# Four interleaved layers (sliding attention, Fourier mixing) on one core: the tables that order both attention layers' half-steps and tails are set anew

## The chip, the core and the metric

The kernel runs on one core of one Trainium2 chip. The core has a matrix engine (PE, with its own queue of weight loads, PEld), a vector engine (DVE), a scalar engine (ACT), GpSimd (POOL), and SP, which only issues transfers. Each engine executes its own instructions in their order in the program and waits at an instruction until what it needs is there. The metric is the time of one execution of the whole program on the device, in microseconds (us); lower is better. Comparisons use the median of several executions.

## What is computed

x has 2048 rows (S) of 640 values (D), in fp32. Four layers are added one after the other: attention A, Fourier mixing B, A, B.

```python
def _A_ref(x, wqkv, wo):
    H = 32; Dh = D // H
    W, dil = 8, 2
    q, k, v = ...                      # from x @ wqkv, 32 heads of 20 values
    idx = pos[:, None] - off[None, :]  # off = 0, 2, .. 14: eight earlier rows
    logits = jnp.einsum("bhsd,bhswd->bhsw", q, kg) * scale
    logits = jnp.where(mask[None, None, :, :], logits, -1e9)
    attn = _softmax(logits, axis=-1)
    o = jnp.einsum("bhsw,bhswd->bhsd", attn, vg)
    return o.transpose(0, 2, 1, 3).reshape(B, S, D) @ wo

def _B_ref(x, ...):
    a = jnp.einsum("bsd,ed->bse", x, dft_hid_re)
    b = jnp.einsum("bsd,ed->bse", x, dft_hid_im)
    return jnp.einsum("ts,bse->bte", dft_seq_re, a) - jnp.einsum("ts,bse->bte", dft_seq_im, b)

x = x + _A_ref(_layernorm(x), A_wqkv, A_wo)
x = x + _B_ref(_layernorm(x), ...)
x = x + _A_ref(_layernorm(x), A_wqkv, A_wo)
x = x + _B_ref(_layernorm(x), ...)
```

## The kernel before

**Products.** A matrix product of fp32 data is done as three products of rounded parts: each operand is kept as a high part (fp32r) and a residue, and high x high, high x residue and residue x high are summed. That is why a projection of a 128-row tile takes 15 matmuls (3 passes of 5 slices of D). To get a tile with D on the partitions, PE transposes it into PSUM (`pc_pe`, L442; `ident` is the identity), ACT casts the result to the high part (`pc_hi`, L446), PE subtracts that high part from what stands in PSUM with a negated identity (`pc_sub`, L450), and ACT or DVE takes the residue out (`pc_lo`, L463 and L465). Between a transpose and its subtraction PE must have other work, or it waits for the cast.

**An attention layer.** The rows are cut into 4 chunks of 4 tiles. `qkv_mm` (L477) projects one tile, for one of four groups of heads, into one of two PSUM banks m0 and m1. ACT evacuates it (`qkv_evac`, L487, L491, L492), and `qkv_store` (L504, L505) writes the keys and values (`kvb`) and the queries (`qb`) of two tiles to DRAM, from the queue of ACT or of SP (`kvq`). For each of 32 units u (a chunk and an eighth of the heads), `q_load` and `w_load` (from SP) bring the queries and the windows of keys and values back; ACT copies the queries (`q_copy`, L530) into a PSUM tile `pq`; DVE multiplies (`qk_mul`, L557) and POOL adds halves (L560); DVE reduces (`qk_red`, L570) and does the softmax (L585 to L595) around ACT's exp (L578); DVE multiplies with the values (`av_mul`, L600) and POOL adds up (`av_tree`, L615 to L617; at the very end DVE shares this). The outputs are transposed as above and multiplied with wo (`wo_mm`, L640); DVE adds the result to x and sums the rows (`wo_add`, L258); ACT takes the variance (L263, L265). The inverse root of the variance comes either from POOL's power (`finish`, L280 and L282, four tiles at once) or from ACT's Ln and Exp (L271, L272), by the table `lno`. Normalisation is on ACT (L297); the cast of the normalised tile to its high part is `ln_hi` (L1044, ACT), its residue `ln_lo` (L1048, on DVE or POOL by the table `lnv`).

**A Fourier layer** starts inside the attention layer before it: `z_mm` (L1123) multiplies normalised tiles with the DFT matrix over the sequence, in thirds of five matmuls, each third a row of the table `z`. The matrix tiles are loaded (`stg<-cst_in`), and their parts made by `c_hi` (L1074) and `c_lo` (L1106), or read back from DRAM (`c_get`). The rest of the layer is eight steps of `pair` with products L1291 and L1190, whose operands DVE and ACT make ready (L1284, L1285), and outputs through `yout` and L331, L342.

**What sets the order.** `layer_a` does not write instructions down directly. It calls `at(step, phase, function, ...)`, which puts the call into a plan. There are about 66 half-steps, two to each unit. The loop that emits them goes through the half-steps, and in each through the phases in the order of one of two strings of `C['ph']` (one up to half-step 47, one from 48 on):

```python
with tc.manual_schedule(engines=ENGINES):
    for s in range(gs[0], last + 1):
        for ph in C["ph"][s >= 48].split():
            for fn, args in plan.pop((s, ph), ()):
                fn(*args)
```

What it emits is the order of all five engines, word for word. `gs` gives the half-step of each `qkv_mm`; `out`, `t2`, `t3` those of the outputs' transposes; `wo`, `w2`, `w3` those of `wo_mm`; `z` those of the thirds (three values to a half-step: phases z0, z1, pe3); `ln` those of the normalisation for the layer after. After the last half-step a string `tail` of letters orders what is left. Entry 0 of `ly` is for the first attention layer (0 to about 400 us), entry 1 for the second (about 865 to 1260 us). At the seam, the first inputs of the second attention layer are made within the last pair of the Fourier layer, at places given by `early`. In the Fourier layers only PE's order is written out (`run`), and the other engines follow a scheduler.

Of the kernel before, what the change touches and what calls it, by code (L numbers as in the profile page):

```python
# [21 lines left out]
H = 32  # L22
# [4 lines left out]
P = 128  # L27
# [25 lines left out]
 'bufs': {'xa': 2, 'qs': 2, 'stg': 2, 'xr': 1},  # L53
 'pad2': 16,
 'ot': ['ot'],
 'wqg': [0, 0, 0, 0, 0, 0, 0, 1, 1, 1, 0, 1, 0, 1, 1, 0, 1, 0, 1, 0],
 'run': [{'pre': [0, 1, 2, 0, 1, 0, 2, 0, 0, 0, 0, 2, 0, 1, 0, 0],
          'post': [5, 1, 1, 2, 1, 4, 0, 5, 0, 7, 0, 3, 0, 4, 1, 5],
          'y': [[3, 4, 5, 6, 8], [9, 13, 14, 14, 15]]},
         {'pre': [6, 0, 1, 2, 4, 3, 0, 4, 0, 6, 0, 0, 2, 0, 0, 0],  # L60
          'post': [0, 0, 2, 2, 0, 4, 0, 0, 0, 0, 1, 0, 4, 0, 4, 3],
# [5 lines left out]
         'ord': [[2, 0, 1, 3, 4, 6, 5, 7], [2, 0, 1, 4, 6, 5, 3, 7], [0, 2, 1, 4, 3, 6, 5, 7]],  # L67
         'out': [20, 23, 27, 32, 36, 40, 44, 47],
         'wo': [21, 22, 26, 26, 29, 30, 33, 34, 38, 39, 42, 42, 45, 47, 49, 49],
         'woph': 'z1',  # L70
         'ln': [40, 43, 44, 47, 53, 53, 55, 55],
         'w2': [52, 53, 54, 55],
         'w3': [60, 61],
         'lnown': [4, 3],
         'z': [148, 149, 149, 151, 151, 156, 156, 157, 157, 159, 161, 162, 167, 168, 170, 171, 171, 173, 174, 174,
               175, 175, 175, 176, 178, 179, 180, 180, 181, 184, 186, 186, 187, 187, 188, 188, 191, 193, 194, 198,
               198, 199],
         'early': [3, 3, 6.5, 8.7, 5, 6, 7, 8.5, 10, 11, 14, 14.1, 8],
# [11 lines left out]
         'ph': ['evac dma peT0 pe hi z0 fin peL z1 red0 pe2 qk dma2 sA sB red1 sC av0 loE sD sE exp actl evacA sF '  # L90
                'evacO av1 qc dmaw dmac actL lnl pe3w dmar misc clo dmas pe3',
                'peT0 evac dma pe hi z0 peL red0 pe2 z1 fin qk dma2 sA av0 sD sE sB red1 evacA sC loE actL sF evacO '
                'exp dmac av1 actl qc dmas misc clo lnl dmar dmaw pe3 pe3w'],
         'xst': 3,
         'xld': 4,
         'lnx': False,
         'lno': [True, False, False, False],
         'whole': [7, 57, 61],
         'lnv': [1, 1, 1, 0, 0, 1, 0, 0, 0, 1, 0, 0, 1, 1, 0, 1],
# [7 lines left out]
         'ord': [[0, 4, 2, 1, 3, 6, 5, 7], [2, 0, 3, 1, 4, 6, 7, 5], [0, 2, 1, 3, 4, 6, 5, 7]],  # L107
         'out': [20, 24, 29, 32, 36, 40, 44, 46],
         'wo': [23, 23, 26, 28, 30, 31, 34, 35, 38, 38, 42, 42, 46, 47, 48, 49],
         'woph': 'z1',  # L110
         'ln': [40, 42, 42, 46, 52, 54, 55, 55],
         'w2': [52, 53, 54, 55],
         'w3': [60, 61],
         'lnown': [4, 2],
         'z': [148, 148, 150, 151, 151, 152, 155, 160, 161, 162, 164, 168, 168, 169, 169, 170, 171, 171, 173, 174,
               175, 175, 177, 178, 178, 179, 179, 180, 181, 183, 185, 185, 186, 186, 187, 188, 188, 188, 191, 192,
               199, 205],
         'early': [5.3, 2.4, 6.1, 8.4, 5.6, 6, 7.3, 8.8, 7.4, 9.0, 13.0, 13.9, 9.3],
         'ym': [-7, 0],
         'ymph': 'pe2',  # L120
         't2': [49, 49, 48, 48, 50, 50, 52, 52],
         't3': [59, 58, 60, 60],
         'wst': [-1, 0, 0, 1, 0, 1, 0, 0, 0, 0, 0, 0, 1, 0, 0, 0],
         'kvq': [1, 1, 1, 0, 0, 0, 0, 0, 1, 0, 0, 0, 0, 1, 0, 0, 1, 0, 0, 0, 0, 0, 1, 0, 0, 0, 0, 0, 0, 0, 1, 0],
         'yd': [1, 1],
         'ymst': [1, 0],
         'cring': ['s3', 's0', 'wa', 's2'],
         'cpe': [0, 0, 0, 0, 0, 0, 0, 0, 0, 0, 0, 0, 0, 0],
         'zla': [0, 0, 2, 0, 1, 0, 1, 1, 1, 1, 0, 1, 0, 2],
         'ph': ['dma peT0 evac hi red0 pe z0 peL qk z1 fin sA pe2 red1 dma2 sB sD sC av0 loE sE clo evacA exp actl '  # L130
                'actL sF evacO av1 qc dmaw dmas misc pe3 lnl dmar dmac pe3w',
                'peT0 red0 evac pe z0 dma hi fin peL sA z1 qk dma2 pe2 sB red1 av0 sD loE evacA sC sE exp actL evacO '
                'sF av1 dmas dmaw qc actl dmar lnl misc pe3w clo dmac pe3'],
         'xst': 3,
         'xld': 4,
         'lnx': True,
         'lno': [False, False, True, True],
         'whole': [32, 61],
         'lnv': [1, 0, 1, 0, 0, 0, 1, 0, 1, 1, 0, 1, 1, 1, 1, 1],
         'kw': {'pc_pe 57': 3, 'pc_pe 54': 1},  # L140
         'tail': 'z68 P H L M2 z67 M3 A2 S2 F2 c14 d14 p14 T2 A3 l2 Z14 z69 S3 F3 c15 d15 p15 T3 l3 G0 G1 G2 Z15 E '
                 'e0 h0 k0 e1 e2 e3 e4 h1 k1'}],
 'xcr': ['stg', 'sg3', 'sg3']}
TA = 65
# [1416 lines left out]
```

## Time and profile before

| what | before |
|---|---|
| median of 3 runs | 1744.4 us (1742.13 to 1746.95) |
| the profiled execution: its time / its span | 1743.01 us / 1741.2 us |
| granted PE clock | 1.0 throughout |
| PE busy | 1717.2 us, 99% |
| DVE, ACT, POOL busy | 78%, 47%, 35% |

The page gives, for each engine, the time in which at least one instruction ran. A row of the timeline has its start, its length, the engine, line, operation, output and inputs, and in brackets how long the engine stood idle before it and what ended this; several like instructions in a row are one row (x4). PE's matmuls overlap, so the distance between starts, not the length, tells what one costs. The table by stretch has for each window the busy time of PE, PEld, DVE, ACT and POOL with the number of instructions, the clock, the share of the DMA engines and GB/s. Whoever wants to know what a change of order is worth looks at two things: where PE is idle and for whom, and how much later than the engine it will meet next it comes there.

### The profile page before, as it was taken

The numbers are of one execution on the slowest core, as the hardware profiler recorded it, in microseconds if no ns is written. First come the engines' busy times: TensorE is split into PE (matmuls) and PEld (weight loads), VectorE is DVE, ScalarE is ACT, GpSimd is POOL, SyncE is SP. The second block draws the span as 40 slices with busy tenths as digits, with TensorE's granted clock in tenths as the row PEclk, the third lists the DMA queues.
The fourth block names the chain that finished last, engine by engine and source line by source line (L and its number), as shares of the span: only waits on it lengthen the run. The fifth ranks groups of instructions, "written<-read, shape, count | busy, mean of one in ns | idle before, by whom it ended". The sixth has DMA issues, their size and how long they took to land. (4 is left out here: it accounts for less than half of the span.)

```text
span 1741.2 us, 26545 instructions
## 1 busy us (share of the span) xinstructions
PE 1717.2 (99%) x8828; PEld 1496.2 (86%) x8828; DVE 1360.1 (78%) x2117; ACT 822.6 (47%) x1810; POOL 616.1 (35%) x574
## 2 busy tenths in 40 slices
PE   9999999999999999999999999999999999999999
PEld 6888888788888888888888889888888888888888
DVE  5999999878767767767639998899787677677673
ACT  5655644654445444445534434445444444443441
POOL 4899999950000000000019997899200000000000
PEclk9999999999999999999999999999999999999999
DMA  6786779969787687687548856698598768867861
GB/s 239 245 291 199 209 231 309 323 222 331 264 262 232 215 275 235 206 279 226 189 156 269 273 163 219 213 312 318 179 349 268 256 205 260 257 208 240 264 203 54
DMA packets 266713, 419.91 MB, mean 241 GB/s; under 512 B 22192, under 2 KB 144560, under 8 KB 266320
## 3 DMA queue, kind: packets, MB, share of 16 engines
q1 hardware_dynamic: 251744, 408.38, 71.1%
q10 hardware_dynamic: 14832, 9.83, 1.8%
q8 instruction: 70, 1.15, 0.3%
q14 instruction: 67, 0.55, 0.1%
HBM read 332.99 MB, written 85.14 MB: 240 GB/s over the span
## 5 line engine op out<-in xcount | busy, mean ns | idle before, releaser
L477 PE MATMUL m<-r,s 128*128 128x512 f32 (+1 forms) x1920 | 429.8, 379 | 1.3 <-DVE r L759 0.8
L477 PEld LDWEIGHTS m<-r,s 128*128 128x128 f32 x1920 | 350.2, 188 | 57.5 <-DVE r L759 1.2
L1284 ACT CAST r<-win 128x512 fp32r<-128x512 f32 x242 | 147.1, 620 | 176.1 <-DVE win L1320 103.2
L1190 PE MATMUL aux<-r2a,zo 128*128 128x320 f32 x768 | 226.0, 309 | 0.0
L557 DVE TENSOR_TENSOR pr<-pq,win 128x1280 f32<-128x1280 f32 x128 | 189.8, 1483 | 37.5 <-PE aux L1190 20.3
L615 POOL TENSOR_TENSOR pr<-pr 128x640 f32<-128x640 f32 x126 | 207.5, 1647 | 30.3 <-DVE pr L600 29.1
L1190 PE MATMUL aux<-pr,zo 128*128 128x320 f32 x704 | 208.0, 309 | 0.0
L560 POOL TENSOR_TENSOR pr<-pr 128x640 f32<-128x640 f32 x123 | 176.3, 1433 | 88.4 <-DVE pr L557 88.4
L1285 DVE TENSOR_TENSOR r<-win,r 128x512 fp32r<-128x512 f32 x242 | 162.8, 688 | 38.5 <-ACT r L1284 37.7
L600 DVE TENSOR_TENSOR pr<-pq,win 128x1280 f32<-128x1280 f32 x128 | 190.3, 1488 | 2.6
L280 POOL TENSOR_TENSOR stats<-stats,mhalf 128x1 f32<-128x1 f32 (+1 forms) x31 | 22.1, 714 | 457.9 <-ACT stats L274 457.8
L1291 PE MATMUL m<-r,r 128*128 128x512 f32 x600 | 152.9, 389 | 0.0
L1190 PEld LDWEIGHTS aux<-r2a,zo 128*128 128x128 f32 x768 | 144.2, 188 | 2.2
L1190 PEld LDWEIGHTS aux<-pr,zo 128*128 128x128 f32 x704 | 132.2, 188 | 2.4
L1291 PEld LDWEIGHTS m<-r,r 128*128 128x128 f32 x600 | 112.2, 188 | 23.5 <-DVE r L1285 0.6
L1291 PE MATMUL t<-r,r 128*128 128x512 f32 x492 | 132.0, 390 | 0.0
L616 POOL TENSOR_TENSOR pr<-pr 128x320 f32<-128x320 f32 x126 | 113.1, 897 | 9.9
L570 DVE TENSOR_REDUCE lg<-pr 128x64 f32<-128x640 f32 (+1 forms) x128 | 107.2, 837 | 10.0 <-POOL pr L560 9.7
L1320 DVE TENSOR_TENSOR win<-win,win 128x512 f32<-128x512 f32 x109 | 74.9, 691 | 48.4 <-DMA win<-cs_in 46.8
L1291 PEld LDWEIGHTS t<-r,r 128*128 128x128 f32 x492 | 92.4, 188 | 19.8
L1123 PE MATMUL m<-s,r 128*128 128x512 f32 x348 | 106.7, 394 | 2.0 <-ACT r L1060 0.9
L1123 PE MATMUL t<-s,r 128*128 128x512 f32 x348 | 105.2, 390 | 0.0
(297 smaller groups left out, 3236.1 us busy)
## 6 DMA issues: line engine op xcount, KB each, us to landing
win<-cs_in SPq DMA_DIRECT2D x346, 256.0 KB, 4.1
r<-xc SPq DMA_DIRECT2D x240, 256.0 KB, 4.2
win<-kvb SPq DMA_DIRECT2D x96, 440.0 KB, 4.7
xa<-cs_in SPq DMA_DIRECT2D x120, 256.0 KB, 4.5
win<-kvb SPq DMA_DIRECT2D x64, 360.0 KB, 6.0
xc<-sg SPq DMA_DIRECT2D x28, 512.0 KB, 4.6
xr<-xs SPq DMA_DIRECT2D x40, 320.0 KB, 3.5
kvb<-stg SPq DMA_DIRECT2D x32, 320.0 KB, 2.7
```

Of the source, the lines that this page charges most:

```text
L477: nc.tensor.matmul(mt[g][:, : GW[q]], st[:, a, k], wq[q][:, b, k], start=n == 0, stop=n == 14)
L557: nc.vector.tensor_tensor(pr, q, wview(u, jp, 0, [[1, FE]]), op=ALU.mult)
L560: nc.gpsimd.tensor_tensor(pv[:, :, 0:10], pv[:, :, 0:10], pv[:, :, 10:20], op=ALU.add)
L570: nc.vector.tensor_reduce(rows(lgs[u], jp), pv.rearrange("p (a h) d -> p a h d", h=HE), axis=AX.X, op=ALU.add,)
L600: nc.vector.tensor_tensor(pr.rearrange("p j w (h d) -> p (j w) h d", d=DH), rows(lgs[u], jp).unsqueeze(3).to_broadcast([P, 2 * W, HE, DH]) ...
L615: g.tensor_tensor(pr[:, :, 0:4], pr[:, :, 0:4], pr[:, :, 4:8], op=ALU.add)
L616: g.tensor_tensor(pr[:, :, 0:2], pr[:, :, 0:2], pr[:, :, 2:4], op=ALU.add)
L1123: self.last = nc.tensor.matmul(self.z[t][k], self.xn[c][:, a, j, k * P : (k + 1) * P], self.ct[s][:, b], start=s == 0 and i == 0, stop=s = ...
L1190: self.last = nc.tensor.matmul(self.ym[e][:, :320], zt[(k, a, ri)][:, j2 * P : (j2 + 1) * P], w[:, e * 320 : (e + 1) * 320], start=(k, a, ...
L1284: nc.scalar.copy(hi, raw)
L1285: nc.vector.tensor_tensor(lo, raw, hi.bitcast(F32), op=ALU.subtract)
L1291: nc.tensor.matmul(bank, w(a, kb), hl[b], start=start and (a, b) == (0, 0), stop=stop and (a, b) == (1, 0),)
```

## The change

Only tables change; no function is touched. In both entries of `ly`, `gs`, `out` or `wo`, `ln`, `z`, `t2`, `early`, `wst` (when a finished x tile is stored), `zla` (how far ahead a DFT tile is loaded), `ph` and `tail` get new values. One swap in `ord` changes the order of two groups of the last chunk's projections in the first layer. `kvq` moves two pairs of stores from ACT's queue to SP's and one the other way. `lnv` moves one residue from POOL to DVE in the first layer and three from DVE to POOL in the second. `lno` makes ACT (Ln, Exp and a small multiplication per tile) instead of POOL finish the statistics of chunk 1 in the second layer. `wqg` sets anew which of DVE and POOL splits some weights (L233: POOL 5 of 25 in place of 6). In `run` some preparations of the Fourier layers' products change their places. The matmuls are the same 8828.

```diff
--- before.py
+++ after.py
@@ -53,92 +53,92 @@
- 'wqg': [0, 0, 0, 0, 0, 0, 0, 1, 1, 1, 0, 1, 0, 1, 1, 0, 1, 0, 1, 0],
...
+ 'wqg': [0, 0, 0, 0, 0, 0, 0, 0, 0, 1, 0, 1, 1, 1, 1, 0, 1, 0, 1, 0],
...
- 'ly': [{'gs': [-7, -6, -5, -4, -3, -2, -1, 0, 1, 2, 3, 3, 4, 5, 5, 6, 6, 7, 8, 8, 9, 11, 11, 12, 13, 13, 14, 15, 16,
...
+ 'ly': [{'gs': [-7, -6, -5, -4, -3, -2, -1, 0, 1, 2, 3, 3, 4, 5, 5, 6, 6, 7, 8, 8, 10, 11, 11, 12, 13, 13, 14, 14, 15,
...
-         'z': [148, 149, 149, 151, 151, 156, 156, 157, 157, 159, 161, 162, 167, 168, 170, 171, 171, 173, 174, 174,
...
+         'z': [149, 149, 150, 151, 151, 155, 156, 156, 156, 157, 161, 162, 165, 168, 170, 171, 172, 172, 173, 173,
...
-         'kvq': [1, 0, 1, 1, 0, 1, 1, 0, 0, 0, 0, 0, 1, 0, 1, 0, 0, 0, 0, 0, 0, 0, 1, 0, 0, 0, 1, 0, 1, 0, 1, 0],
+         'kvq': [1, 0, 1, 1, 0, 0, 1, 0, 0, 0, 0, 1, 1, 0, 1, 0, 0, 0, 0, 0, 0, 0, 0, 0, 0, 0, 1, 0, 1, 0, 1, 0],
...
-                'peT0 evac dma pe hi z0 peL red0 pe2 z1 fin qk dma2 sA av0 sD sE sB red1 evacA sC loE actL sF evacO '
-                'exp dmac av1 actl qc dmas misc clo lnl dmar dmaw pe3 pe3w'],
...
+                'peT0 evac dma pe hi z0 peL red0 pe2 z1 fin qk dma2 sA av0 sD sE sB red1 evacA sC loE actL sF evacO '
+                'exp dmac av1 actl misc qc dmas clo lnl dmar dmaw pe3 pe3w'],
...
-         'lnv': [1, 1, 1, 0, 0, 1, 0, 0, 0, 1, 0, 0, 1, 1, 0, 1],
...
+         'lnv': [1, 1, 1, 0, 0, 1, 0, 0, 1, 1, 0, 0, 1, 1, 0, 1],
...
-                'peT0 red0 evac pe z0 dma hi fin peL sA z1 qk dma2 pe2 sB red1 av0 sD loE evacA sC sE exp actL evacO '
-                'sF av1 dmas dmaw qc actl dmar lnl misc pe3w clo dmac pe3'],
...
+                'peT0 red0 evac pe z0 dma hi fin peL sA z1 qk dma2 pe2 sB evacA red1 sD av0 loE sC exp sE actL evacO '
+                'sF av1 dmas dmaw qc actl dmar dmac lnl misc pe3w clo pe3'],
...
-         'lno': [False, False, True, True],
...
+         'lno': [False, True, True, True],
...
-         'lnv': [1, 0, 1, 0, 0, 0, 1, 0, 1, 1, 0, 1, 1, 1, 1, 1],
...
+         'lnv': [0, 0, 1, 0, 0, 0, 1, 0, 1, 1, 0, 0, 1, 1, 0, 1],
```

Three places in the order. First, PE in the first attention layer at about 84 to 88 us: projections (L477; `s_115`, `s_133` are the transposed tiles 1 and 2), then the transposes of tile 3 (`xa_742`) and their subtraction (L450). Before:

```order
L477 MATMUL m_137_886<-r_0_12_157,s_115_744 128x512 x15
L477 MATMUL m_143_928<-r_0_12_157,s_133_856 128x512 x15
L442 MATMUL xt_975<-ident_69,xa_742 128x128 x4
L442 MATMUL t_153_976<-ident_69,xa_742 128x128
L450 MATMUL xt_975<-s_151_974,nident_74 128x512
L450 MATMUL t_153_976<-s_151_974,nident_74 128x128
L477 MATMUL m_158_1006<-r_0_12_157,s_151_974 128x512 x15
```

Now:

```order
L477 MATMUL m_137_885<-r_0_12_157,s_115_744 128x512 x15
L442 MATMUL xt_955<-ident_69,xa_742 128x128 x4
L442 MATMUL t_150_956<-ident_69,xa_742 128x128
L477 MATMUL m_151_962<-r_0_12_157,s_133_856 128x512 x15
L450 MATMUL xt_955<-s_148_954,nident_74 128x512
L450 MATMUL t_150_956<-s_148_954,nident_74 128x128
L477 MATMUL m_158_1006<-r_0_12_157,s_148_954 128x512 x15
```

The transposes have moved ahead of one burst of 15 projections, and that burst now lies between them and their subtraction. A like move is made at about 108 us.

Second, PE in the same layer at about 324 to 329 us: transposes of an output piece (`zo`) and of a DFT tile just loaded (`stg`), a third of `z_mm` with the DFT tile `wa`, and the subtractions. Before (a second third with `wa` follows, and then the subtractions):

```order
L442 MATMUL aux_585_3695<-ident_69,zo_520_3259 128x128 x3
L442 MATMUL aux_587_3697<-ident_69,stg_3667 128x128 x4
L1123 MATMUL m_496_3155<-wa_3645,r_1_539_3391 128x512
L1123 MATMUL m_497_3156<-wa_3645,r_1_539_3391 128x512
L1123 MATMUL xt_3157<-wa_3645,r_1_539_3391 128x512
L1123 MATMUL t_499_3158<-wa_3645,r_1_539_3391 128x512
L1123 MATMUL t_500_3159<-wa_3645,r_1_539_3391 128x512
```

Now (another third with `wa` stands ahead of these rows):

```order
L1123 MATMUL m_503_3180<-wa_3597,r_1_539_3392 128x512
L1123 MATMUL m_504_3181<-wa_3597,r_1_539_3392 128x512
L1123 MATMUL xt_3182<-wa_3597,r_1_539_3392 128x512
L1123 MATMUL t_506_3183<-wa_3597,r_1_539_3392 128x512
L1123 MATMUL t_507_3184<-wa_3597,r_1_539_3392 128x512
L442 MATMUL aux_585_3706<-ident_69,zo_522_3267 128x128 x3
L442 MATMUL aux_587_3708<-ident_69,stg_3673 128x128 x4
L450 MATMUL aux_585_3706<-s_584_3705,nident_74 128x384
L450 MATMUL aux_587_3708<-s_586_3707,nident_74 128x512
```

Both thirds stand ahead of the transposes, and the subtractions follow right behind them.

Third, ACT in the second attention layer at about 1060 to 1071 us: evacuations of projections (L491, L492), the exp of unit 16 (L578), the normalisation of an input tile (L297) and the copy of the queries (L530). Before:

```order
L491 COPY stg_10690<-m_1515_10650 128x6x80
L492 COPY sg_1457_10255<-m_1515_10650 128x2x16
L491 COPY stg_10740<-m_1524_10696 128x6x80
L492 COPY sg_1528_10739<-m_1524_10696 128x2x16
L578 ACTIVATE lg_10666<-lg_10666 128x128
L297 ACTIVATE xa_10551<-xa_10551,stats_8520 128x640
L530 COPY pq_8726<-qs_10686 128x320
L446 CAST s_1538_10787<-xt_10788 128x512
L446 CAST s_1538_10787<-t_1540_10789 128x128
```

Now:

```order
L491 COPY stg_10672<-m_1513_10631 128x6x80
L492 COPY sg_1453_10212<-m_1513_10631 128x2x16
L491 COPY stg_10672<-m_1522_10676 128x6x80
L492 COPY sg_1453_10212<-m_1522_10676 128x2x16
L578 ACTIVATE lg_10650<-lg_10650 128x128
L297 ACTIVATE xa_10551<-xa_10551,stats_8517 128x640
L491 COPY stg_10774<-m_1524_10696 128x6x80
L492 COPY sg_1533_10773<-m_1524_10696 128x2x16
L530 COPY pq_8726<-qs_10668 128x320
```

The exp and the normalisation have moved ahead of the third evacuation.

More of the change, by code (lines that the diff above doesn't have):

```diff
@@ L55 @@
  'ot': ['ot'],
- 'wqg': [0, 0, 0, 0, 0, 0, 0, 1, 1, 1, 0, 1, 0, 1, 1, 0, 1, 0, 1, 0],
[L57 to L61, printed above, removed]
[4 rows of a table removed]
+ 'wqg': [0, 0, 0, 0, 0, 0, 0, 0, 0, 1, 0, 1, 1, 1, 1, 0, 1, 0, 1, 0],
+ 'run': [{'pre': [3, 1, 2, 0, 1, 0, 2, 0, 0, 0, 0, 2, 0, 1, 0, 0],
+          'post': [3, 2, 1, 0, 1, 4, 0, 5, 0, 9, 0, 1, 0, 4, 3, 3],
+          'y': [[3, 4, 4, 6, 8], [11, 13, 13, 14, 15]]},
+         {'pre': [5, 1, 1, 2, 4, 4, 0, 4, 0, 6, 0, 0, 2, 0, 0, 0],
+          'post': [1, 0, 1, 2, 0, 3, 0, 0, 0, 0, 2, 0, 3, 0, 4, 3],
[4 rows of a table added]
          'tx': [4, 6, 8, 10, 15, 18, 20, 22, 30, 32, 34, 36],
-         'ord': [[2, 0, 1, 3, 4, 6, 5, 7], [2, 0, 1, 4, 6, 5, 3, 7], [0, 2, 1, 4, 3, 6, 5, 7]],
-         'out': [20, 23, 27, 32, 36, 40, 44, 47],
-         'wo': [21, 22, 26, 26, 29, 30, 33, 34, 38, 39, 42, 42, 45, 47, 49, 49],
+         'ord': [[2, 0, 1, 3, 4, 6, 5, 7], [2, 0, 1, 4, 6, 5, 3, 7], [2, 0, 1, 4, 3, 6, 5, 7]],
+         'out': [20, 25, 27, 32, 35, 40, 44, 47],
+         'wo': [21, 22, 26, 26, 29, 30, 33, 34, 38, 39, 42, 42, 45, 46, 49, 49],
          'woph': 'z1',
@@ L89 @@
          'zla': [0, 0, 0, 0, 0, 0, 0, 2, 0, 0, 1, 0, 1, 0],
[L90 to L91 removed]
+         'ph': ['evac dma peT0 pe hi fin z0 peL pe2 red0 z1 qk dma2 sA sB red1 sC av0 loE sD sE exp actl evacA sF '
+                'evacO av1 qc dmaw dmac actL pe3w dmar misc clo lnl dmas pe3',
                 'peT0 evac dma pe hi z0 peL red0 pe2 z1 fin qk dma2 sA av0 sD sE sB red1 evacA sC loE actL sF evacO '
[L93 removed]
+                'exp dmac av1 actl misc qc dmas clo lnl dmar dmaw pe3 pe3w'],
          'xst': 3,
```

34 lines of the change are left out of this document (17 added, 17 removed), and 12 rows, old and new, of the table CFG.

## Prediction

> **What bounds the kernel now.** I read the page's busy times first, then the table by stage, then the waits of the tensor engine, and last the timeline at each of those waits.
>
> ```profile
> span 1741.2 us, 26545 instructions
> PE 1717.2 (99%) x8828; PEld 1496.2 (86%) x8828; DVE 1360.1 (78%) x2117; ACT 822.6 (47%) x1810; POOL 616.1 (35%) x574
> ```
>
> The change leaves all 8828 matmuls in place, so only the 24.0 us in which PE is idle (1741.2 - 1717.2) can go, or grow. The rows by stretch (length, then busy time of PE, PEld, DVE, ACT, POOL, clock) say where they lie:
>
> ```profile
> 325.00:350.00 25.00, 22.72 (x120) 19.25 (x121) 22.30 (x29) 13.60 (x32) 24.06 (x21) 1.00 0.92 323
> 600.00:625.00 25.00, 25.00 (x112) 20.68 (x111) 18.11 (x30) 11.66 (x23) 0.00 (x0) 1.00 0.91 296
> 1150.00:1175.00 25.00, 22.45 (x134) 20.38 (x133) 23.51 (x38) 10.30 (x28) 23.82 (x23) 1.00 0.92 317
> ```
>
> The Fourier layers (600 to 625 stands for them) leave PE no gap. The attention layers do (2.3 of 25 us at 325, 2.6 at 1150), and there DVE and POOL have 22 to 24 of 25 us of work as well. So in these two stages three engines run nearly level, and a matmul moved into a gap pays only as far as the vector work can follow. No PE wait is long; two rows of the list of PE's waits (total, times, longest):
>
> ```profile
> PE aux L450 <- ACT r L446: 1.7, 2, 1.6
> ...
> PE aux L442 <- DMA stg<-cst_in: 1.7, 1, 1.7
> ```
>
> L442 transposes, L446 casts on ACT, L450 subtracts the cast from the transposed piece: a round trip PE to ACT to PE that only other matmuls between the two can cover.
>
> **The first attention layer (0 to 400 us).** The timeline of PE at the waits that the new order touches:
>
> ```profile
> 87.20 0.50 PE L450 MATMUL xt<-s,nident 128*128 128x512 f32 x1 [0.68 <-ACT s L446]
> ...
> 108.39 0.66 PE L442 MATMUL xt<-ident,xa 128*128 128x128 f32 x4 [0.92 <-ACT xa L297]
> ...
> 286.16 0.50 PE L450 MATMUL aux<-wa,nident 128*128 128x512 f32 x1 [0.40 <-ACT wa L446]
> ...
> 287.33 0.66 PE L442 MATMUL aux<-ident,zo 128*128 128x128 f32 x4 [0.46 <-ACT wa L465]
> ...
> 325.94 0.63 PE L442 MATMUL aux<-ident,stg 128*128 128x128 f32 x4 [1.69 <-DMA stg<-cst_in]
> ...
> 332.54 0.62 PE L1123 MATMUL m<-s,r 128*128 128x512 f32 x2
> ...
> 333.68 0.60 PE L442 MATMUL aux<-ident,stg 128*128 128x128 f32 x4
> 334.95 0.50 PE L450 MATMUL aux<-s,nident 128*128 128x512 f32 x1 [0.68 <-ACT s L446]
> ```
>
> At 87.20 the transposes now stand ahead of a burst of 15 matmuls instead of behind it; a 512-wide matmul takes 0.23 us (five of them, one third of a z product, lie between 332.54 and 333.68), so 3.4 us now lie between transpose and subtraction, more than the 0.68 us that were lacking: -0.68. At 108.39 another such burst goes ahead of transposes that wait for the normalised input: -0.92. At 284 to 291 the transposes of two half chunks are merged and a third of a z product is put between: the waits of 0.40 and 0.46 are covered, but the subtraction of the first piece now follows its transposes with only four others between, and a bare round trip costs 0.68 by the 334.95 row, of which the four (0.60 in the 333.68 row, overlapping) cover all but some 0.2: -0.86 + 0.2, about -0.7. At 325.94 two thirds (ten matmuls, 2.3 us) go ahead of the transposes that wait 1.69 us for a constant's load, -1.69; they stood behind these transposes and covered their cast, so that round trip is bare now, +0.68. At 334.95 a third comes between: -0.68. The sum of PE terms is -0.68 - 0.92 - 0.7 - 1.69 + 0.68 - 0.68 = -4.0 us.
>
> They can't all be kept. The stage ends when PE transposes the last attention outputs, and the vector side finishes them only shortly before:
>
> ```profile
> 370.96 0.54 DVE L617 TENSOR_TENSOR zo<-pr 128x160 f32<-128x160 f32 x1
> ...
> 373.26 0.60 PE L442 MATMUL pq<-ident,zo 128*128 128x128 f32 x4
> ```
>
> From 371.50 (370.96 + 0.54) to 373.26 are 1.76 us: PE can come that much earlier and no more, unless DVE ends earlier too. On DVE two things change. The stores of one K/V and Q block (L504, L505) go from ACT's queue to SP's, and behind them ACT copies the q that DVE waits for:
>
> ```profile
> 190.45 0.43 ACTq L504 DMA_DIRECT2D kvb<-stg  x1
> 190.92 0.54 ACTq L505 DMA_DIRECT2D qb<-stg  x1
> ...
> 199.91 1.49 DVE L557 TENSOR_TENSOR pr<-pq,win 128x1280 f32<-128x1280 f32 x1 [1.03 <-ACT pq L530]
> ```
>
> That is at most -0.97 (0.43 + 0.54, within the 1.03). One residue of the next layer's input (L1048, ln_lo) goes from POOL to DVE: +0.82 by the 816 ns row below. DVE's end moves by -0.15, so the cap is about 1.9. I take **-2.0** for this layer; its bounds are 0 (PE's gains are waited off at the next anchor) and -4.0 (every PE term kept). POOL's relief by the same residue is taken as nothing, since the sum at 370.96 is DVE's.
>
> **The second attention layer (865 to 1260 us).** Here the largest edit is on ACT. The exp of unit 16 and a normalisation stood behind an evacuation that waits for PE; they now stand ahead of it:
>
> ```profile
> 1067.04 0.56 ACT L491 COPY stg<-m 128x480 f32<-128x480 f32 x1 [2.75 <-PE m L477]
> ...
> 1067.57 0.32 ACT L578 ACTIVATE lg<-lg 128x128 f32<-128x128 f32 x1
> ...
> 1067.92 0.29 DVE L591 TENSOR_REDUCE pq<-lg 128x16 f32<-128x128 f32 x1 [3.24 <-ACT lg L578]
> ```
>
> So DVE's wait of 3.24 us goes: the evacuation at 1067.04 had kept ACT idle for 2.75 us. Against it, another normalisation of 0.94 us falls out of an idle stretch of ACT into the copy that DVE waits for at 1049.04:
>
> ```profile
> 1045.22 0.94 ACT L297 ACTIVATE xa<-xa,stats 128x640 f32<-128x640 f32 x1
> ...
> 1049.04 1.49 DVE L557 TENSOR_TENSOR pr<-pq,win 128x1280 f32<-128x1280 f32 x1 [2.36 <-ACT pq L530]
> ```
>
> DVE is up by 2.3 us (3.24 - 0.94). Its waits between 1020 and 1120 (total, times, longest) are nearly all for ACT:
>
> ```profile
> DVE pr L557 <- ACT pq L530: 6.1, 5, 2.4
> DVE pq L591 <- ACT lg L578: 4.7, 2, 3.2
> ```
>
> The copies in the first row stand behind evacuations that PE paces, and a DVE that comes earlier waits there longer, so I let most of the 2.3 be waited off. What PE can gain lies at 1148 to 1164:
>
> ```profile
> 1148.37 0.55 PE L442 MATMUL aux<-ident,zo 128*128 128x128 f32 x3 [0.25 <-POOL zo L617]
> ...
> 1156.88 0.50 PE L450 MATMUL aux<-r,nident 128*128 128x256 f32 x2 [1.57 <-ACT r L446]
> ...
> 1163.92 2.32 PE L640 MATMUL aux<-r2a,s 128*128 128x320 f32 x14 [0.98 <-DVE r L258]
> ```
>
> Transposes that waited 0.25 for POOL come later (-0.25). A third of z (five matmuls, 1.1 us) that stood ahead of the 1163.92 row is now ahead of the 1156.88 row: -1.1 there, +1.1 at 1163.92 unless DVE's add (L258) comes earlier. On POOL the two statistics instructions ahead of the half-sums of unit 26, 1.01 and 0.20 us, become small ACT instructions, while three residues go from DVE to POOL. The cap is again the end of the vector side:
>
> ```profile
> 1229.73 0.54 DVE L617 TENSOR_TENSOR zo<-pr 128x160 f32<-128x160 f32 x1
> ...
> 1231.54 0.60 PE L442 MATMUL pq<-ident,zo 128*128 128x128 f32 x4
> ```
>
> It leaves 1.27 us (1231.54 - 1230.27). I take **-1.0**: 0.25 at 1148, and some 0.75 where DVE's lead shortens the 0.98 at 1163.92. Bounds: +1.0 (the third gives 1.1 back and nothing is earlier) and -2.8 (0.25 + 1.57 + 0.98).
>
> The residues have these prices:
>
> ```profile
> L1048 POOL TENSOR_TENSOR r<-r,r x10: 1569/1578/1589, 307.9 to 1201.2; 128x640 fp32r<-128x640 f32 x10
> L1048 DVE TENSOR_TENSOR r<-xa,r x9: 815/816/1273, 237.0 to 1222.4; 128x640 fp32r<-128x640 f32 x9
> L1048 DVE TENSOR_TENSOR r<-r,r x6: 954/1455/2004, 305.0 to 1202.2; 128x640 fp32r<-128x640 f32 x6
> ```
>
> On DVE the same 128x640 takes 0.82 at best and 2.00 at worst, on POOL always near 1.58. I book the three moves in the second layer as -0.82 each for DVE, hidden by the waits above, and as covered on POOL by the 1.21 us of statistics and its slack to 1231.54; without that cover POOL would end 3 x 1.58 - 1.21 = 3.5 us later. The Trainium skill (GPSIMD Engine Reference, Specifications) speaks against such moves: VectorE and GpSimd share the interfaces to SBUF, and DVE instructions with two SBUF inputs contend. The trace bears it out as far as the spread of 0.82 to 2.00 us goes, though no row names the cause.
>
> **Edits taken as nothing.**
>
> ```profile
> L1285 DVE TENSOR_TENSOR r<-win,r 128x512 fp32r<-128x512 f32 x242 | 162.8, 688 | 38.5 <-ACT r L1284 37.7
> ```
>
> The seam (847 to 930) keeps its PE order; the later load and the copy of the first q lie under the Fourier layer's last products. The Fourier layers' own tables move casts and combines of DVE and ACT while PE is busy 25.00 of 25.00; without that cover each late combine would cost its 0.69 us (L1285). The tails move allocations and one load. Their bound is 1 us either way.
>
> **Sum.** -2.0 - 1.0 = -3.0. The profiled execution took 1743.0 us (span 1741.2), so it becomes 1740.0; the median of the runs shown, 1744.4, lies 1.4 above it, which gives **1741.4 us**. About 0.3%, 5.2 us, is what a measurement of this kernel can tell from no change.
>
> **Rivals.**
> First, the caps give way: DVE's lead of 2.3 us survives to 1164 and both sides end earlier, so the PE terms are kept whole: -4.0 - 2.8 = -6.8, 1737.6 us. For it speaks that the 6.1 and 4.7 us of DVE's waits are for ACT, whose order is what changes; against it the 1.76 and 1.27 us.
> Second, slower: in the first layer two pairs of stores go to SP's queue and one leaves it. SP also issues the window loads for DVE's products; a store that waits for its evacuation holds the loads behind it. The loads' landing time, and DVE's wait for them between 50 and 375:
>
> ```profile
> win<-kvb SPq DMA_DIRECT2D x96, 440.0 KB, 4.7
> ...
> DVE pr L557 <- DMA win<-kvb: 0.7, 1, 0.7
> ```
>
> Where a store stands ahead of a load with no lead left, DVE, busy 23 of 25 us, can't catch up: 4.7 for each of two, less the 1.76 of slack, less the 1.0 of the second layer: +6.6, 1751.0. Before, DVE waited for such a load 0.7 us in all, so there was a lead; it decides once the held loads lose more than it.
> Third, contention: each of the three residues moved to POOL stretches a DVE product beside it by 1.18 (2.00 - 0.82), 3.5 together, in place of the -1.0: -2.0 + 3.5 = +1.5, 1745.9. By the skill's rule on the shared interfaces this is what off-loading to POOL would do.
> Fourth, nothing moves, because each PE gain is waited off at the next anchor of DVE (L258) or of a load: 1744.4.
>
> **How the numbers follow.** Forecast 0.36, first rival 0.30, second 0.16, third 0.08, fourth 0.10. The forecast's own range is 1739 to 1744. For the first rival's spread the range goes down to 1735.5 (a further 2.1, DVE's whole lead kept), and up to 1748, which leaves out most of the second. Faster by over 0.3% is under 1739.2: most of the first rival (0.26) and over a quarter of the forecast (0.10), 0.36. Slower by over 0.3% is over 1749.6: the second rival and a little of the third, 0.17. The rest, 0.47, is within.
>
> **What would show it.** In the new trace the waits at 87, 108 and 326 us are gone and new ones of some 0.7 us stand behind the transposes near 285 and 328. DVE's wait of 3.2 us for exp near 1067 is gone, the one near 1049 is longer. PE's total idle is near 21 us. If the gap between the last sums (L617) and PE's transposes at the end of each attention layer has shrunk from 1.8 and 1.3 us to nearly nothing, the cap was real; if it stayed and the end came earlier, the first rival holds. I am wrong on the other side if DVE shows waits of microseconds for `win<-kvb`, or if PE's idle rises over 24 us.

## The result, and the profile after

| | before | changed |
|---|---|---|
| median of 22 runs each | 1742.62 us | 1740.62 us |
| lowest to highest | 1741.09 to 1747.63 | 1739.14 to 1742.87 |
| span of the profiled execution | 1741.2 us | 1739.3 us |

The ratio of changed to before is 0.9984, with a 95% interval of 0.9978 to 0.9991: 2.8 us faster, between 1.6 and 3.8. The two medians are 2.0 us apart. The forecast was 3.0 us. When the changed kernel was timed again (below), the executions with a granted clock of 1.0 alone had medians of 1742.93 before (21 of 33) and 1740.68 changed (8 of 11), so the gain is not one of the clock.

The page of the changed kernel, its first rows:

```profile
span 1739.3 us, 26562 instructions
PE 1718.1 (99%) x8828; PEld 1496.7 (86%) x8828; DVE 1356.2 (78%) x2116; ACT 825.3 (47%) x1818; POOL 616.4 (35%) x573
```

PE is idle for 21.2 us (1739.3 - 1718.1) where it was 24.0. The span fell by less, 1.9 us, since the same 8828 matmuls count as busy for 0.9 us longer (1718.1 - 1717.2). By stretch (length, then busy PE, PEld, DVE, ACT, POOL, clock), two windows of the attention layers:

```profile
325.00:350.00 25.00, 24.09 (x132) 20.43 (x131) 23.61 (x32) 13.02 (x29) 24.05 (x22) 1.00 0.95 348
1150.00:1175.00 25.00, 23.34 (x140) 21.33 (x139) 23.42 (x41) 14.91 (x38) 23.59 (x21) 1.00 1.00 374
```

These windows have gained 1.4 and 0.9 us of PE work (22.72 and 22.45 before). The list of PE's waits (total, times, longest) has another head:

```profile
PE m L477 <- ACT sg L492: 1.5, 1, 1.5
...
PE aux L442 <- DVE r L258: 1.1, 1, 1.1
PE aux L640 <- DVE r L258: 1.1, 1, 1.1
```

None of these three was among the first three of before. The timeline of PE shows where they stand:

```profile
105.68 0.62 PE L477 MATMUL m<-r,s 128*128 128x384 f32 x2 [1.54 <-ACT sg L492]
...
284.18 0.63 PE L442 MATMUL aux<-ident,zo 128*128 128x128 f32 x4 [0.63 <-DVE xa L258]
285.54 0.39 PE L450 MATMUL aux<-ot,nident 128*128 128x256 f32 x1 [0.30 <-ACT s L446]
...
304.43 0.66 PE L442 MATMUL aux<-ident,stg 128*128 128x128 f32 x4 [1.09 <-DVE r L258]
...
326.64 0.60 PE L442 MATMUL aux<-ident,stg 128*128 128x128 f32 x4
327.37 1.05 PE L450 MATMUL aux<-s,nident 128*128 128x384 f32 x2
328.26 0.64 PE L1123 MATMUL m<-wa,r 128*128 128x512 f32 x2
...
333.32 0.39 PE L450 MATMUL aux<-s,nident 128*128 128x512 f32 x1
```

The waits at 87, 108, 326 and 335 us of before are gone. New are the 1.54 at 105.68 and 0.87 more at 304.43. Rows of before to compare:

```profile
304.72 0.66 PE L442 MATMUL aux<-ident,stg 128*128 128x128 f32 x4 [0.22 <-DVE r L258]
...
326.32 0.70 PE L1123 MATMUL m<-wa,r 128*128 128x512 f32 x2
...
328.71 0.56 PE L450 MATMUL aux<-s,nident 128*128 128x384 f32 x2
329.11 0.63 PE L1123 MATMUL m<-wa,r 128*128 128x512 f32 x2
```

The move behind 326 us did bare a round trip, though the row at 327.37 has no bracket. From the four transposes at 326.64 to the next z matmul at 328.26 PE now takes 1.62 us. Before, when other matmuls lay between, the same four transposes took 0.38 (325.94 to 326.32) and the two subtractions 0.40 (328.71 to 329.11). The difference, 0.84 us, is spread over this row and shows only in the distances between starts.

Single profiles differ by some tenths of a microsecond in each layer, so every profile below is read by the same two stretches, between PE instructions that stand at the same place of the program in all of them. Before, the first layer's stretch goes from the subtraction at 58.66 to the z matmul at 384.91, the second layer's from 1138.78 to 1242.89:

```profile
58.66 0.50 PE L450 MATMUL xt<-s,nident 128*128 128x512 f32 x1 [0.68 <-ACT s L446]
...
384.91 1.35 PE L1123 MATMUL m<-s,r 128*128 128x512 f32 x3 [0.59 <-ACT r L1060]
...
1138.78 0.44 PE L450 MATMUL t<-r,nident 128*128 128x384 f32 x1 [0.24 <-ACT r L446]
...
1242.89 0.73 PE L1123 MATMUL m<-s,r 128*128 128x512 f32 x2 [0.29 <-ACT r L1060]
```

In the changed kernel:

```profile
58.64 0.51 PE L450 MATMUL xt<-s,nident 128*128 128x512 f32 x1 [0.67 <-ACT s L446]
...
383.07 2.06 PE L1123 MATMUL m<-s,r 128*128 128x512 f32 x6 [0.59 <-ACT r L1060]
...
1137.05 0.44 PE L450 MATMUL t<-r,nident 128*128 128x384 f32 x1 [0.24 <-ACT r L446]
...
1239.80 2.07 PE L1123 MATMUL m<-s,r 128*128 128x512 f32 x6 [0.32 <-ACT r L1060]
```

So the first stretch fell from 326.25 to 324.43 us (-1.82) and the second from 104.11 to 102.75 (-1.36). The last Fourier layer gives 1.2 back: PE is 3.09 us ahead at 1239.80 (1242.89 - 1239.80) and 1.9 at the end. Two PE waits stand there that the kernel before did not have:

```profile
1319.23 0.94 PE L1291 MATMUL t<-r 128*128 128x512 f32 x3 [0.71 <-DVE ot L1169]
...
1416.85 0.73 PE L1291 MATMUL xt<-s,r 128*128 128x512 f32 x2 [0.42 <-DVE s L1285]
```

### The profile page after: what moved, and what is told of

The parts are those of the page before. It is cut to its first block, busy times and chain, and to the rows that moved or that the text cites. A ratio compares the mean times of both kernels' runs of the same rounds, so it can differ in the third digit from the quotient of the medians.

```text
span 1739.3 us, 26562 instructions
## 1 busy us (share of the span) xinstructions
PE 1718.1 (99%) x8828; PEld 1496.7 (86%) x8828; DVE 1356.2 (78%) x2116; ACT 825.3 (47%) x1818; POOL 616.4 (35%) x573
## 4 chain that ended last, share of the span: by engine, by line
PE 81%; DVE 9%; POOL 4%; issue 2%; DMA 2%; ACT 2%; ACTq 0%; SPq 0%; DVEq 0%; POOLq 0%
PE m L477 16%; PE aux L1190 15%; PE t L1291 11%; PE m L1291 11%; PE aux L640 6%; PE pq L1291 5%; PE xt L1291 5%; PE m L1123 4%; PE t L1123 4%; DVE pr L557 2%; PE xt L1123 2%; DVE pr L600 2%; POOL pr L615 1%; POOL pr L560 1%; DMA win<-cs_in 1%
## 5 line engine op out<-in xcount | busy, mean ns | idle before, releaser
L477 PE MATMUL m<-r,s 128*128 128x512 f32 (+1 forms) x1920 | 430.1, 379 | 2.8 <-ACT sg L492 1.5
L477 PEld LDWEIGHTS m<-r,s 128*128 128x128 f32 x1920 | 350.1, 188 | 59.3 <-ACT sg L492 2.8
L557 DVE TENSOR_TENSOR pr<-pq,win 128x1280 f32<-128x1280 f32 x128 | 189.8, 1482 | 38.9 <-PE aux L1190 20.3
L600 DVE TENSOR_TENSOR pr<-pq,win 128x1280 f32<-128x1280 f32 x128 | 190.3, 1488 | 2.7
```

Source lines behind the costliest of these rows:

```text
L477: nc.tensor.matmul(mt[g][:, : GW[q]], st[:, a, k], wq[q][:, b, k], start=n == 0, stop=n == 14)
L557: nc.vector.tensor_tensor(pr, q, wview(u, jp, 0, [[1, FE]]), op=ALU.mult)
L600: nc.vector.tensor_tensor(pr.rearrange("p j w (h d) -> p (j w) h d", d=DH), rows(lgs[u], jp).unsqueeze(3).to_broadcast([P, 2 * W, HE, DH]) ...
```

## The experiments

`CFG` is the dictionary of tables; `before` and `after` are those of the two kernels. Each kernel was profiled once, "store pair 11 on SP" twice; some were also timed against the kernel before. The intervals of the ratios are some 0.1% wide on each side, 1.7 us, so the stretches decide most of what follows. All stretches, in us:

| kernel | first stretch | second stretch | ratio to before (95% interval) |
|---|---|---|---|
| before | 326.25 | 104.11 | |
| changed | 324.43 | 102.75 | 0.9984 (0.9978 to 0.9991) |
| changed, again | 324.79 | 103.36 | 0.9989 (0.998 to 0.9998) |
| old Fourier tables | 324.77 | 102.69 | 0.999 (0.9981 to 0.9999) |
| first layer's tables only | 325.14 | 103.35 | 0.9992 (0.9983 to 1.0001) |
| second layer's tables only | 325.99 | 103.87 | 0.9999 (0.9991 to 1.0008) |
| four thirds back | 325.92 | 102.78 | 1.0 (0.9991 to 1.0009) |
| store pair 11 on SP | 323.07; 323.87 | 103.55; 105.14 | 0.9979 (0.9967 to 0.9991) |
| projection 20 back | 325.05 | 103.28 | |
| projection 47 back | 325.04 | 103.18 | |
| residue back on POOL, first layer | 325.33 | 103.49 | |
| residues back on DVE, second layer | 324.76 | 103.81 | |
| statistics back on POOL, second layer | 324.68 | 103.94 | |

Seven profiles share the changed kernel's first layer (changed, again, Fourier, first only, projection 47, second layer's residues, statistics): 324.43 to 325.14, mean 324.80. The two with the old one have 326.12 on average. The first layer is worth about 1.3 us, and one profile tells a difference of 0.7 us, not of 0.3.

This stretch can be cut at PE's wait for DVE's add near 304 us. In every profile 1288 matmuls lie ahead of this wait and 401 behind it. Ahead of it, the two profiles with the old tables take 246.06 and 245.67 us and the seven with the new ones 245.79 to 246.43: nothing is won there. Behind it, the old ones take 80.19 and 80.32 and the new ones 78.59 to 78.76. So the layer's gain, 1.6 us behind the wait less some 0.3 ahead of it, lies wholly behind the wait, where it is far clear of the spread.

The second layer is noisier: eight profiles with its full new tables and a clock of 1.0 in this stretch give 102.69 to 103.87, mean 103.22, the two with the old tables 104.11 and 103.35. About 0.5 us; the two sets overlap. Cut at PE's wait for DVE's add near 1161 us (to within one matmul, 0.15 us), the part behind it is steadier: 78.97 in both profiles with the old tables, 78.35 to 78.40 in seven of the eight with the new ones and 78.76 in the eighth. Ahead of it, 25.14 and 24.38 with the old tables and 24.31 to 25.15 with the new tell no difference.

### One layer alone, the Fourier tables, and a control

```diff
 CFG = before
+CFG['ly'][0] = after['ly'][0]
+CFG['wqg'] = after['wqg']
```

> The kernel before with the new tables of the first attention layer alone (entry 0 of ly, and wqg); the second layer and both Fourier layers keep theirs. Theory (each layer's gain is its own): PE is 1.8 us earlier at 400 us, as in the changed kernel, and stays so to the end: a ratio to before near 0.9990, with no new wait of PE after 1260 us. Rival (the gain of the second layer feeds on the first layer's, or the first layer's gain is waited off at the seam): PE is earlier by 1.8 us at 400 but by less than 0.5 at 1000, and the time is that of before.

The first stretch is 325.14, 1.1 us under before where 1.8 were expected, and 1742.53 us stands against 1743.11; the interval of the ratio holds 1, so the time alone does not show it. PE stays ahead by 1.0 us up to 1135. The lead is not waited off at the seam.

```diff
 CFG = before
+CFG['ly'][1] = after['ly'][1]
```

> The kernel before with the new tables of the second attention layer alone (entry 1 of ly). Theory (each layer's gain is its own): no shift up to 860 us, PE 1.4 us earlier at 1240 us, and with the Fourier layers' old tables nothing is given back after it: ratio near 0.9992. Rival: without the first layer's change the second brings nothing (ratio 1.000).

The second stretch is 103.87, only 0.2 under before, and the time is the same. This is the weakest of the eight profiles, so the run neither shows a gain of the second layer alone nor excludes the 0.5.

```diff
 CFG = after
+CFG['run'] = before['run']
```

> The changed kernel with the Fourier layers' old tables (run) put back. In the changed kernel PE has new waits of 0.7 us at 1319 (L1291 for a DVE cast or combine) and 0.4 us at 1417, and gives back 1.2 us of its lead after 1260. Theory (the new tables of the last Fourier layer make them): both are gone and the time is about 1.0 us under the changed kernel's, ratio to before near 0.9978. Rival (they come and go with the landing of loads from run to run, whatever the table): they stay or stand elsewhere, and the ratio is 0.9984 as before.

Both waits are gone, and the time is that of the control below (1741.13 and 1741.07 us): the first half of the theory came, the second did not.

```diff
 CFG = after
```

> The changed kernel once more, as a control: a second profile of the same program. If the order of the program decides the waits, the same PE waits stand at the same places, 1.5 us at 105.7, 1.1 at 304.4, 1.1 at 1161.4, 0.7 at 1319 and 0.4 at 1417, within 0.2 us each; if the landing of loads decides those after 1260 us, the last two differ by more than that. Ratio 0.9984 within 0.0006.

The waits at 105.7 (1.54), 304 (1.40) and 1161 (1.08) are there again. Those at 1319 and 1417 are not. So what the Fourier layer gave back belonged to that one execution, not to its tables; the rival holds. This profile also shows where 3 us can go that have nothing to do with the order. Its first rows by stretch:

```profile
0.00:25.00 25.00, 21.25 (x74) 13.13 (x75) 14.60 (x30) 12.32 (x30) 6.44 (x17) 0.86 0.68 252
25.00:50.00 25.00, 25.00 (x112) 20.69 (x111) 10.85 (x14) 13.71 (x35) 11.66 (x10) 1.00 0.58 179
```

PE's granted clock was 0.86 in the first 25 us, and PE reached the first mark at 61.89 where the changed kernel's first profile has 58.64.

### The largest term of the first layer

```diff
 CFG = after
-CFG['ly'][0]['z'][16:20] = [172, 172, 173, 173]
+CFG['ly'][0]['z'][16:20] = [171, 173, 174, 174]
```

> The changed kernel with four of its z thirds in the first layer put back (the two with wa stand behind the transposes again, not ahead of them; the load, casts and residue of their DFT tile move back with them). Theory (this move is the largest kept term of the first layer): the wait of about 1.7 us for the DFT tile's load near 325 us is back, the bare round trips near 327 are gone, and PE's lead between 145 and 400 us, 1.4 to 1.8 in the changed kernel, shrinks by 1.0 to 1.3. Rival (the cap: the vector engines set the end of the layer, and this PE term was waited off): the lead shrinks by less than 0.3 and the gap between DVE's last sum (L617) and PE's transposes near 371 us, 1.78 us in the changed kernel, is shorter by a microsecond.

The first stretch is 325.92: of the 1.3 us, 1.1 are lost again, and the ratio is 1.0. Most of it, 0.9 us, is lost behind the wait at 304 (79.59 against 78.65, the mean of the seven). The wait for the load is shorter than expected, and another has come back at 334 (PE):

```profile
324.89 0.63 PE L442 MATMUL aux<-ident,stg 128*128 128x128 f32 x4 [0.42 <-DMA stg<-cst_in]
...
334.03 0.50 PE L450 MATMUL aux<-s,nident 128*128 128x512 f32 x1 [0.44 <-ACT s L446]
```

The gap between the last sum and PE's transposes is 1.76 us here too (PE 372.89, DVE 370.59 + 0.54), so the rival with the cap falls.

### The new wait at 105.7

```diff
 CFG = after
-CFG['ly'][0]['kvq'][11] = 1
+CFG['ly'][0]['kvq'][11] = 0
```

> The changed kernel with one pair of stores (number 11 of the first layer) on SP's queue again instead of ACT's. Theory: the new PE wait of 1.54 us at 105.7 is ACT's evacuation, held by a staging buffer whose store has not landed, and this pair, issued at 99.0 beside another pair of SP's, is the reason that the store lands late: the wait shrinks by 0.5 us or more. What is won is waited off by 305 us, where PE waits for DVE's add: the lead at 400 us stays within 0.3 of the changed kernel's 1.4 to 1.8. Rival (the wait is of the projections' order alone): 1.5 us stays.

ACT in the changed kernel (issues of its DMA queue included):

```profile
99.01 0.41 ACTq L504 DMA_DIRECT2D kvb<-stg  x1
99.46 0.58 ACTq L505 DMA_DIRECT2D qb<-stg  x1
...
104.98 0.56 ACT L491 COPY stg<-m 128x480 f32<-128x480 f32 x1 [1.62 <-DMA qb<-stg]
```

The other pair of stores, from SP's queue at the same time, and DVE:

```profile
99.69 1.09 SPq L505 DMA_DIRECT2D qb<-stg  x1
...
115.03 1.49 DVE L557 TENSOR_TENSOR pr<-pq,win 128x1280 f32<-128x1280 f32 x1 [1.25 <-ACT pq L530]
```

The evacuation waits until a staging buffer (`stg`, two of them) has been stored. PE waits for the evacuation, and 10 us later DVE waits 1.25 us for ACT's copy of q. With the pair on SP's queue, SP, ACT, PE and DVE:

```profile
100.01 1.08 SPq L505 DMA_DIRECT2D qb<-stg  x1
...
103.91 0.56 ACT L491 COPY stg<-m 128x480 f32<-128x480 f32 x1 [0.24 <-DMA qb<-stg]
...
104.61 5.50 PE L477 MATMUL m<-r,s 128*128 128x384 f32 x30 [0.17 <-ACT sg L492]
...
114.01 1.48 DVE L557 TENSOR_TENSOR pr<-pq,win 128x1280 f32<-128x1280 f32 x1
```

The wait is nearly gone, as expected. The second half of the expectation fell: the win was not waited off by 305. The first stretch is 323.07, 1.7 under the mean of the changed kernel. All of it lies ahead of the wait at 304 (244.46 us there, where the seven have 245.79 or more), and DVE's wait at 115 is gone.

The store was not alone in making that wait. ACT's copy of q stands behind a cast (L446) of the transposes that moved behind a burst of projections near 108 us. This cast started at 109.09 before, at 110.58 with the pair on SP's queue and at 111.62 in the changed kernel. So the burst had used up ACT's lead, and the store went beyond it. No run puts that burst back. The run with the pair on SP's queue was tried again and timed:

> The changed kernel with store pair 11 of the first layer on SP's queue, timed. In one profile the wait at 105.7 us was gone, DVE's wait of 1.25 us for the copy of q at 115.0 with it, and DVE and PE stayed 1.0 us further ahead to 380 us. Theory (this pair on ACT's queue cost the changed kernel 1.0 us on DVE's chain, and this chain sets the pace up to 300 us): the lead at 380 over that at 60 is 2.5 to 2.9 us, the time 1.0 under the changed kernel's, ratio to before 0.9975 to 0.9985. Rival (the lead is waited off in the Fourier layer): lead as said, ratio as for the changed kernel, 0.9984 to 0.9990.

The first stretch is 323.87, 2.4 under before (326.25 - 323.87) where 2.5 to 2.9 were expected. The time, 1739.99 us against 1742.3, has a ratio of 0.9979 (0.9967 to 0.9991): faster than before, but its interval holds the changed kernel's 0.9984, so the microsecond is shown by the profiles alone. The second stretch of this profile, 105.14, is left out of the mean, for its clock was 0.93 there:

```profile
1150.00:1175.00 25.00, 22.53 (x127) 20.74 (x126) 22.61 (x37) 13.38 (x34) 23.11 (x20) 0.93 0.98 349
```

### A term ahead of that wait

```diff
 CFG = after
-CFG['ly'][0]['gs'][20] = 10
+CFG['ly'][0]['gs'][20] = 9
```

> The changed kernel with one burst of projections a half-step earlier, so that the transposes at 86 us stand right ahead of their subtraction again. Theory (the 0.68 us won there is lost at the wait at 105.7, which ends with the landing of a store): the wait of 0.68 near 87 us is back, the one at 105.7 falls from 1.54 to about 0.9, and the lead at 145 us stays within 0.2 of zero. Rival (the term is kept): the wait at 105.7 stays 1.5 and PE is 0.7 later at 145 and at 380.

PE:

```profile
87.14 0.50 PE L450 MATMUL xt<-s,nident 128*128 128x512 f32 x1 [0.68 <-ACT s L446]
...
105.89 1.34 PE L477 MATMUL m<-r,s 128*128 128x384 f32 x6 [1.10 <-ACT sg L492]
```

Of the 0.68 us won at 87 in the changed kernel, 0.44 (1.54 - 1.10) were lost at 105.7, and the first stretch, 325.05, is within the spread of the changed kernel's. The term brought nothing that can be seen.

### Exp ahead of the evacuation, residues, statistics

```diff
 CFG = after
-CFG['ly'][1]['gs'][47] = 34
+CFG['ly'][1]['gs'][47] = 33
```

> The changed kernel with one projection of the second layer a half-step earlier again, so that the exp of unit 16 stands behind the third evacuation once more. Theory (the gain of 3.2 us on DVE is waited off behind PE's evacuations): DVE's wait for exp near 1066 is 3 us again, DVE's waits for copies of q between 1020 and 1120 fall from 9.0 to about 6 us, and PE's lead at 1136 and at 1238 us moves by less than 0.3. Rival (DVE's lead from there is what shortened the waits near 1160): PE at 1238 is later by 0.7 to 1.5.

DVE's waits between 1020 and 1120 in the changed kernel (total, times, longest):

```profile
DVE pr L557 <- ACT pq L530: 9.0, 5, 3.4
DVE pq L591 <- ACT lg L578: 2.8, 2, 1.4
```

With the projection, and so the exp, back:

```profile
DVE pr L557 <- ACT pq L530: 7.9, 5, 3.2
DVE pq L591 <- ACT lg L578: 3.9, 2, 2.4
```

The sum is 11.8 us in both, against 10.8 (6.1 + 4.7) before the change: what is saved at one copy of ACT is waited at the next. The second stretch, 103.18, does not move. The waits moved less than expected (2.4 where 3 was said, 7.9 where 6).

```diff
 CFG = after
-CFG['ly'][0]['lnv'][8] = 1
+CFG['ly'][0]['lnv'][8] = 0
```

> The changed kernel with the residue of the first layer that had gone to DVE back on POOL. If DVE sets the end of the first layer, DVE's last sum and PE's end of the layer come 0.5 to 0.8 us earlier. If PE's own order sets it, nothing moves by more than 0.3. If POOL, which then has 1.58 us more, sets it, the end comes up to 1.6 later.

The first stretch is 325.33, 0.2 over the spread and 0.5 over the mean. It is not earlier, so taking the residue (0.82 us at 324 in the changed kernel) off DVE wins nothing; whether POOL makes it later can't be told from one profile.

```diff
 CFG = after
-CFG['ly'][1]['lnv'][0], CFG['ly'][1]['lnv'][11], CFG['ly'][1]['lnv'][14] = 0, 0, 0
+CFG['ly'][1]['lnv'][0], CFG['ly'][1]['lnv'][11], CFG['ly'][1]['lnv'][14] = 1, 1, 1
```

> The changed kernel with the three residues of the second layer back on DVE. Theory (0.82 us each off DVE's chain, of which part is kept): PE's lead between 1056 and 1238 us, 0.85 to 1.42 in the profiles with the new tables, falls by 0.4 to 0.9. Rival (contention: POOL beside DVE stretches DVE's products as much): it stays or grows.

The second stretch is 103.81, 0.6 over the mean, on the side that the theory said, but within the eight profiles' spread. Contention would have made it shorter. The pages speak on this rival by themselves. The row of DVE's products (L600) before and in the changed kernel:

```profile
L600 DVE TENSOR_TENSOR pr<-pq,win 128x1280 f32<-128x1280 f32 x128 | 190.3, 1488 | 2.6
...
L600 DVE TENSOR_TENSOR pr<-pq,win 128x1280 f32<-128x1280 f32 x128 | 190.3, 1488 | 2.7
```

They took 1488 ns on average in both, and none of the 128 took more than 1.50 us. The products of L557 are as even (1483 and 1482 ns). So no product was stretched by 1.18 us.

```diff
 CFG = after
-CFG['ly'][1]['lno'][1] = True
+CFG['ly'][1]['lno'][1] = False
```

> The changed kernel with the statistics of chunk 1 of the second layer finished by POOL's power again. Theory (1.21 us on POOL ahead of the half-sums of unit 26, hidden only in part): the wait of PE for DVE's add near 1161 us, 1.08, grows to 1.5 to 2.3 and the lead between 1056 and 1238 falls by 0.4 to 1.2. Rival (POOL has slack there): 1.08 stays within 0.2 and so does the lead.

POOL and PE:

```profile
1156.18 1.01 POOL L280 TENSOR_TENSOR stats<-stats,mhalf 128x4 f32<-128x4 f32 x1
...
1162.53 1.73 PE L640 MATMUL aux<-r2a,s 128*128 128x320 f32 x10 [1.81 <-DVE r L258]
```

The wait grew from 1.09 to 1.81, as the theory said, and the stretch to 103.94, 0.7 over the mean. Moving these statistics to ACT is the one part of the second layer for which both a wait and the stretch speak, though from one profile, and with the stretch only 0.07 us above the eight (103.94 against 103.87).

## Why the prediction was right, and where its steps were not

**The size and the side** were right: 3.0 us forecast, 2.8 by the ratio, 2.0 by the medians, 1.9 in the control (0.9989). So was what bounds the kernel: PE's idle time fell to 21.2, where near 21 was said, and the Fourier layers and the seam, booked at nothing, show no gain of their own (old Fourier tables: the control's time). That the total came so close is partly luck. By the stretches the two layers gave 1.3 and 0.5 us where 2.0 and 1.0 were forecast. And the absolute figure, 1741.4 us against 1740.62, starts from 1744.4, a median of three executions that lies 1.8 above the median of the 22.

**First layer, -2.0 forecast, about -1.3 measured.** The prediction's terms behind 304 us are -1.69 + 0.68 - 0.68, -1.7 together, and 1.6 us were won there; with four thirds back, 0.9 of it is lost. The +0.68 for a bared round trip came, as 0.84. The terms ahead of 304, at 87, 108 and 284 to 291 (-0.68 - 0.92 - 0.7 = -2.3), came at their places (at 284 to 291, 0.86 turned into 0.30), and nothing of them is left at 304.

The step that failed is the one on the stores. It priced a pair that leaves ACT's queue (the wait of 1.03 at 199.91 is gone) and left out pair 11, which goes onto it. The runs showed that this pair holds a staging buffer, then an evacuation, then PE for 1.54 us at 105.68, and DVE 10 us later. It costs about 1.3 us (324.80 against 323.07 and 323.87), ahead of 304.

**The cap** was put at the wrong place. By the prediction the gap at the end of the first layer should have shrunk from 1.76 us. DVE and PE in the changed kernel:

```profile
369.10 0.54 DVE L617 TENSOR_TENSOR zo<-pr 128x160 f32<-128x160 f32 x1
...
371.42 0.60 PE L442 MATMUL pq<-ident,zo 128*128 128x128 f32 x4
```

It is 1.78 (371.42 - 369.64): both ends came earlier together. PE's gains are checked further up, where PE waits for DVE's add: 0.22 us at 304.72 before, 1.09 at 304.43 now and 1.40 in the control, so of all that PE had won by then 0.29 us (304.72 - 304.43) were left in one profile and nothing on average. Up to there only what DVE wins counts, as pair 11 shows. Behind it the matmuls put into gaps count: the changed kernel has no later PE wait for an add of DVE before the mark at the end, and there DVE waits for PE's products.

**Second layer, -1.0 forecast, about -0.5 measured, not sharply.** That the 3.24 us ahead of exp would be waited off was right. The 0.75 us expected at the add near 1163.92 did not come (0.98 before, 1.09 now). In the changed kernel's first profile the 1.57 at 1156.88 shrank instead, to 0.40 and 0.16:

```profile
1154.80 0.38 PE L450 MATMUL aux<-ot,nident 128*128 128x256 f32 x1 [0.40 <-ACT ot L446]
1155.34 0.50 PE L450 MATMUL aux<-r,nident 128*128 128x256 f32 x2 [0.16 <-ACT r L446]
1161.40 1.88 PE L640 MATMUL aux<-r2a,s 128*128 128x320 f32 x11 [1.09 <-DVE r L258]
```

In this profile the third of z that filled it was not given back at 1161, since DVE's add came earlier too. Over all profiles the part ahead of 1161 shows no gain. The steady part, 0.6 us, lies behind it: a PE wait for a cast of ACT (L450 for L446), 0.35 us in both profiles with the old tables (at 1191.77 before), stands in none with the new ones. The prediction does not name it, and it does not come back in any run that undoes a part of this layer, so which edit removed it stays open. So the second layer's gain did not come where it was booked. The statistics, taken as covered, are not quite: without their move PE's wait at DVE's add is 0.7 us longer. The three residues, booked at 0.82 us each on DVE, took 0.81, 1.12 and 0.82 there in the run that put them back.

**The rivals.** By the prediction's own sign, a gap that stayed and an end that came earlier, the first rival holds at the end of the first layer, but not in size: of its 6.8 us about 2 came. The fourth, each gain waited off at DVE's next add, holds ahead of 304 us. Loads behind stores on SP did not cost anything that shows: SP issued the load of q at 105.79 where it had been 103.55, but DVE's wait of 0.7 us for `win<-kvb` is 0 to 0.5 in the profiles with the new tables. Stores did cost, but through ACT and the staging buffers. Contention did not show: DVE's products took 1488 ns on average before and after, and with the residues back on DVE the layer is not shorter. By the Trainium skill (GPSIMD Engine Reference, Specifications) DVE and GpSimd share their way to SBUF; no run here shows a price of it for these moves.

## What to carry to other kernels

When two engines run nearly level, find the instruction at which one waits for the other: matmuls put into gaps ahead of it win nothing, and those behind it are kept. Price every store that changes its queue by the buffer that it frees, not only by its issue. And before a microsecond is put down to an edit, profile the same program a second time.

## What the runs showed of the hardware

The store of one staging buffer, issued at 99.46 us on ACT's queue beside another pair on SP's at the same time (99.69), let the evacuation go only at 104.98, 5.5 us later. With both pairs one behind the other on SP's queue, it was issued at 100.01 and the evacuation went at 103.91, 3.9 us later.

The residue of a 128x640 tile (L1048) took DVE 0.82 to 2.00 us and POOL always near 1.58, while DVE's 128x1280 products (L557, L600) never took more than 1.50 us.

Two profiles of one program differ by waits of up to 0.9 us in the Fourier layers (0.93 at 486.03 in one of the two with the pair on SP's queue, 0.71 at 1319.23 in one of the two of the changed kernel; the other of each two has no such wait there). They differ by the granted clock too, which was 0.86 in the first 25 us of two of the 14 profiles and 0.93 in one window of another. The low clock at the start took about 3 us (61.89 against 58.64 at the first mark, in two profiles of the same program), which no order explains.
